# Two weight loads moved to ScalarE's queue, and one more chunk divided in token order, in a two-layer linear-attention kernel

## The chip, the cores and the metric

One core of a Trainium2 chip. The metric is the device time of one execution in microseconds (us), as the median of several executions. All runs quoted here are of the same state (fast).

## The reference, cut to what matters

```python
def _A_ref(x, wqkv, wo):                       # linear attention, 32 heads of 16
    q, k, v = split(x @ wqkv)
    phi = lambda t: where(t > 0, t + 1, exp(t)) + 1e-6
    pq, pk = phi(q), phi(k)
    kv  = einsum("bhsd,bhse->bhde", pk, v)
    z   = einsum("bhsd->bhd", pk)
    num = einsum("bhqd,bhde->bhqe", pq, kv)
    den = einsum("bhqd,bhd->bhq", pq, z)[..., None] + 1e-6
    return (num / den) @ wo                    # heads merged again

def _B_ref(x, w1, b1, w2, b2):                 # norm, w1, gelu, w2
    ...
x = x + _A_ref(norm(x), wqkv, wo);  x = x + _B_ref(norm(x), ...)     # layer 0
x = x + _A_ref(norm(x), wqkv, wo);  x = x + _B_ref(norm(x), ...)     # layer 1, same weights
```

x is 2048 tokens x 512 channels, the inner width of the second block is 1792, everything is bf16 outside.

## The kernel before

The program is scheduled by hand: a list per engine fixes the order of every operation (`ORDER`), a table says where an operation with a choice runs (`WAY`). A small planner walks these lists with a fixed duration for each operation; from that it takes the PSUM bank of every product (PSUM is the memory that TensorE's products go to; the program uses eight banks of it) and the semaphore waits, by which one engine waits for another. Tokens are handled in 16 tiles of 128, in four chunks. Tiles count from 0: the "fourth tile" is tile 3, and it is the fifth to be transposed. Where the prediction says "fourth transpose", it means that of tile 4, which comes just before.

The names that matter below: `PTA0_3` is the transpose on TensorE of the normalised tile 3 of layer 0, `tcA0_3` the copy of it out of PSUM by ScalarE, `K0_3` its four key products, `G0_3_0` its four products of normalised input and phi(k). `D` products make denominators, `ZR1` spreads layer 1's key sum over the partitions, `M1_x` joins the key-value matrix with the output weights, `WO1_x` is the attention's output, `PTB1_x` the second norm's transpose, `W11_...` the first MLP product of layer 1.

The loads at the start, and the two late weights (cut):

```python
dma("sp",  x0)                         # 128 KB, x tile 0
dma("act", x1)                         # 384 KB, x tiles 1 to 3
dma("sp",  wqkv[:, :, D:2*D])          # wk, 512 KB
load_chunk("act", 1, -98)              # 512 KB each
dma("act", wqkv[:, :, 0:D])            # wq, 512 KB
load_chunk("act", 2, -96)
load_chunk("act", 3, -95)
...
if st == 0:                            # after the first transposed tile has been copied
    late("wv", "wv", wqkv[:, :, 2 * D:3 * D], wsrc[:, :, 2 * D:3 * D], -88, 512, [tr])   # GpSimd issues
    late("wo", "wo", wo[:], A_wo.rearrange("(dt p) c -> p dt c", p=P), -87, 512, [tr])
```

The orders in the head (cut):

```
pe:   warm PTA0_0 PTA0_1 K0_0 K0_1 PTA0_2 PTA0_4 K0_2 G0_0_0 PTA0_3 ...
act:  x1 xc1 wq xc2 xc3 tcA0_0 tcA0_1 expk0_0 reluk0_0 tcA0_2 ...
pool: id0 id1 bdm0 neghalf b1z powA0_0 powA0_1 wv powA0_2 vepsA0_4 powA0_4 wo vepsA0_3 powA0_3 ...
dve:  ones statsA0_0 aggrA0_0 vepsA0_0 statsA0_1 statsA0_2 aggrA0_1 normA0_0 vepsA0_1 ...
```

The division by the denominators has two forms, chosen for each chunk (cut):

```python
if by_token(L, c):                                        # token order
    pool/dve: lr = pq * zrow                              # pz
    dve:      rd = reduce_add(heads(lr))                  # red
    dve:      rd = rd + 1e-6                              # den, 128x32
    dve:      rr = reciprocal(rd)                         # rec
    pool/dve: pq = pq * rr                                # pr
    sp:       DMA transpose of pq
else:                                                     # channel order
    pe:  d = zb^T pq                                      # D, 128x512
    act: lr = exp(-ln(d + 1e-6))                          # two instructions
    pool/dve: pq = pq * lr                                # pr
```

## Time and profile before

| | before |
|---|---|
| median of the first three runs | 330.97 us (330.16 to 331.24) |
| span of the profiled run | 328.4 us |
| TensorE busy | 320.1 us, 97% |
| first transpose starts / fourth tile's transpose starts | 6.02 / 12.67 us |
| last product ends | 325.90 us |

The profile's views are shown and read in the prediction below. One rule carries most of the reading: the modelled ends of pipelined matmuls overlap, so a stall of TensorE is read from starts. In this kernel a 512-wide product starts 0.216 us after the one before it; whatever the distance has above that is a stall (or half rate, at which it is 0.427 us; see e10).

A second view of the kernel before: ScalarE's part of the timeline up to its first copy. Columns: start, duration, engine (ACTq is the issue of a transfer by ScalarE), line, operation, output <- input, count, and in brackets the idle time before it and what ended it.

```profile
1.83 0.53 ACTq L626 DMA_DIRECT2D wqkv<-in_A_wqkv_dram  x1
2.39 1.22 ACTq L614 DMA_DIRECT2D t<-in_A_x_dram  x2
6.46 0.60 ACT L729 ACTIVATE t<-ps 128x512 bf16<-128x512 bf16 x1 [4.38 <-PE ps L719]
```

The last of five issues ends at 3.61 us, and the first copy waits for TensorE's transpose.

### The profile page before, as it was taken

The numbers are of one execution on the slowest core, as the hardware profiler recorded it, in microseconds if no ns is written. First come the engines' busy times: TensorE is split into PE (matmuls) and PEld (weight loads), VectorE is DVE, ScalarE is ACT, GpSimd is POOL, SyncE is SP. The second block draws the span as 40 slices with busy tenths as digits, with TensorE's granted clock in tenths as the row PEclk, the third lists the DMA queues.
The fourth block names the chain that finished last, engine by engine and source line by source line (L and its number), as shares of the span: only waits on it lengthen the run. The fifth ranks groups of instructions, "written<-read, shape, count | busy, mean of one in ns | idle before, by whom it ended". The sixth has DMA issues, their size and how long they took to land.

```text
span 328.4 us, 4737 instructions
## 1 busy us (share of the span) xinstructions
PE 320.1 (97%) x1696; PEld 159.1 (48%) x1726; DVE 211.9 (65%) x475; ACT 202.1 (62%) x343; POOL 146.8 (45%) x237
## 2 busy tenths in 40 slices
PE   6899999999999999999999999999999999999996
PEld 2344544576444444444444444458644444444444
DVE  5987757993664567564168889999688985300122
ACT  3899599588873764238974595859955250864300
POOL 4774566767335212753126725856654274000000
PEclk9999999999999999999999999999999999999999
DMA  7833770215022100322020200012033313300012
GB/s 257 271 65 66 229 254 0 50 29 69 17 47 45 22 1 18 64 48 48 2 48 0 50 17 1 18 32 51 16 82 80 79 21 80 96 0 2 16 44 68
DMA packets 45555, 19.71 MB, mean 60 GB/s; under 512 B 39196, under 2 KB 44572, under 8 KB 45532
## 3 DMA queue, kind: packets, MB, share of 16 engines
q1 hardware_dynamic: 41964, 12.21, 17.3%
q0 software_dynamic: 1056, 4.72, 4.2%
q10 hardware_dynamic: 2512, 2.49, 2.3%
q8 instruction: 13, 0.21, 0.3%
q14 instruction: 10, 0.08, 0.1%
HBM read 8.00 MB, written 2.10 MB: 31 GB/s over the span
## 4 chain that ended last, share of the span: by engine, by line
PE 90%; DVE 3%; ACT 2%; DMA 2%; issue 1%; POOL 0%
PE ps L1045 29%; PE ps L1083 28%; PE ps L1013 8%; PE ps L770 8%; PE ps L865 4%; PE ps L801 4%; PE ps L788 3%; PE ps L897 2%; DMA t<-in_A_x_dram 2%; PE ps L1070 1%; PE ps L989 1%; ACT eb L740 1%; DVE gtb L910 1%; PE ps L719 1%; PE ps L846 0%
## 5 line engine op out<-in xcount | busy, mean ns | idle before, releaser
L1051 ACT ACTIVATE gT<-ps,b1c 128x512 bf16<-128x512 f32 (+1 forms) x140 | 76.9, 601 | 56.9 <-PE ps L1045 53.0
L1045 PE MATMUL ps<-t,w 128*128 128x512 bf16 (+1 forms) x552 | 101.2, 336 | 0.3
L1083 PE MATMUL ps<-w,gT 128*128 128x512 bf16 x426 | 97.7, 379 | 0.5
L1045 PEld LDWEIGHTS ps<-t,w 128*128 128x128 bf16 x560 | 54.5, 98 | 43.7 <-ACT t L729 0.3
L1083 PEld LDWEIGHTS ps<-w,gT 128*128 128x128 bf16 x434 | 42.5, 98 | 50.3
L740 ACT ACTIVATE eb<-ps 128x512 bf16<-128x512 f32 x64 | 36.9, 602 | 8.4 <-PE ps L770 4.5
L683 POOL TENSOR_TENSOR rstd<-veps,neghalf 128x1 f32<-128x1 f32 x64 | 37.1, 585 | 6.5 <-DVE veps L681 3.0
L1093 DVE TENSOR_TENSOR outb<-ps,xsb 128x512 bf16<-128x512 f32 x15 | 10.3, 689 | 39.9 <-PE ps L1083 25.7
L671 DVE BATCH_NORM_STATS2 stats<-xsb 128x6 f32<-128x512 f32 x48 | 31.8, 679 | 0.3
L770 PE MATMUL ps<-wqkv,t 128*128 128x512 bf16 x125 | 31.1, 379 | 0.2
L751 ACT ACTIVATE rb<-ps 128x512 bf16<-128x512 f32 x45 | 26.6, 605 | 7.5 <-PE ps L770 3.9
L1013 PE MATMUL ps<-gtb,t 128*128 128x512 bf16 x125 | 30.6, 379 | 0.4 <-DVE gtb L881 0.2
L691 ACT ACTIVATE yb<-xsb,nmr,rstd 128x512 bf16<-128x512 f32 x21 | 16.9, 810 | 16.0 <-POOL nmr L688 15.9
L757 POOL TENSOR_TENSOR t<-eb,rb 128x512 bf16<-128x512 bf16 x14 | 16.8, 1201 | 12.2 <-DVE eb L753 7.5
L696 DVE TENSOR_SCALAR yb<-xsb,mv,rstd 128x512 bf16<-128x512 f32 x27 | 15.5, 578 | 8.8 <-POOL rstd L683 8.6
L997 POOL TENSOR_TENSOR t<-t,lr 128x512 bf16<-128x512 bf16 x13 | 15.3, 1180 | 12.7 <-ACT lr L993 12.3
L681 POOL TENSOR_SCALAR veps<-mv 128x1 f32<-128x1 f32 x29 | 8.0, 279 | 27.6 <-DVE mv L673 26.9
L753 DVE TENSOR_SCALAR eb<-eb 128x512 bf16<-128x512 bf16 x45 | 14.6, 333 | 8.5 <-ACT eb L740 8.5
L1089 DVE TENSOR_TENSOR xsb<-ps,xsb 128x512 f32<-128x512 f32 x16 | 11.0, 690 | 13.5 <-PE ps L1083 13.5
L1013 PEld LDWEIGHTS ps<-gtb,t 128*128 128x128 bf16 x128 | 12.4, 98 | 14.7 <-DVE gtb L881 0.7
L1213 ACT ACT_TABLE_LOAD x15 | 19.2, 1283 | 0.3
L770 PEld LDWEIGHTS ps<-wqkv,t 128*128 128x128 bf16 x128 | 12.1, 98 | 14.6 <-ACT t L729 0.6
(91 smaller groups left out, 390.5 us busy)
## 6 DMA issues: line engine op xcount, KB each, us to landing
w<-in_B_w_dram POOLq DMA_DIRECT2D x4, 896.0 KB, 7.0
out_dram<-outb SPq DMA_DIRECT2D x15, 128.0 KB, 1.8
t<-in_A_x_dram ACTq DMA_DIRECT2D x3, 512.0 KB, 8.3
t<-yb SPq DMA_TRANSPOSE x55, 2.5
wqkv<-in_A_wqkv_dram SPq DMA_DIRECT2D x1, 512.0 KB, 5.6
wqkv<-in_A_wqkv_dram ACTq DMA_DIRECT2D x1, 512.0 KB, 7.3
wqkv<-in_A_wqkv_dram POOLq DMA_DIRECT2D x1, 512.0 KB, 6.3
wo<-in_A_wo_dram POOLq DMA_DIRECT2D x1, 512.0 KB, 5.0
```

Source lines behind the costliest of these rows:

```text
L671: G.op("dve", lambda e: e.bn_stats(stats[:, s.slot, :], src()), 620, reads=src_keys, writes=[k + "s"], tiles=[s, *src_tiles], prio=prio, n ...
L683: G.op("pool", lambda e: e.tensor_tensor(rstd[:, s.slot:s.slot + 1], veps[:, s.slot:s.slot + 1], neghalf[:], op=ALU.pow), 570, reads=[k + ...
L691: G.op("act", lambda e: e.activation(yb[:, y.slot, :], src(), ACT.Identity, bias=nmr[:, s.slot:s.slot + 1], scale=rstd[:, s.slot:s.slot + 1]),
L740: G.op("act", lambda e: e.activation(eb[:, et.slot, :], bank(bt), ACT.Exp), 478, reads=[src_key], writes=[f"e{tag}"], tiles=[bt, et], prio ...
L751: G.op("act", lambda e: e.activation(rb[:, rt.slot, :], bank(bt), ACT.Relu), 478, reads=[src_key], writes=[f"r{tag}"], tiles=[bt, rt], pri ...
L757: lambda e: e.tensor_tensor(dst(), eb[:, et.slot, :], rb[:, rt.slot, :], op=ALU.add),
L770: ins = e.matmul(bank(b), lhsT=yTa(yT)[:, dt, k * P:(k + 1) * P], rhs=wqkv[:, dt, D:2 * D], start=(dt == 0), stop=(dt == DT - 1))
L1013: ins = e.matmul(bank(wb), lhsT=yTa(pq)[:, kt, k * P:(k + 1) * P], rhs=gtb[:, kt, :], start=(kt == 0), stop=(kt == DT - 1))
L1045: ins = e.matmul(bank(b, n), lhsT=w1[:, dt, ft * P:(ft + 1) * P], rhs=yTa(yT)[:, dt, k0 * P:k1 * P], start=(dt == 0), stop=(dt == DT - 1))
L1051: G.op("act", lambda e, ft=ft, b=b, k0=k0, k1=k1, n=n: e.activation(gT[:, g.slot, ft * 512 + k0 * P:ft * 512 + k1 * P], bank(b, n), ACT.Ge ...
L1083: ins = e.matmul(bank(b), lhsT=gT[:, g.slot, ft * 512 + k * P:ft * 512 + (k + 1) * P], rhs=w2[:, ft, :], start=(ft == 0), stop=(ft == FT - 1))
L1213: e.preload_act_table_set(sets[table])
```

## The change

The intent: take the two issues off GpSimd, where they stand between the norms that the first transposes wait for, and take four products and a transpose off TensorE, the engine that bounds the kernel. All orders and some 75 placements were redone along with it. The core of the diff, orders and placements cut:

```diff
         load_chunk("act", 3, -95)
+        dma("act", lambda e: e.dma_start(wqkv[:, :, 2 * D:3 * D], wsrc[:, :, 2 * D:3 * D]), ["wv"], prio=-94, name="wv", kb=512)
+        dma("act", lambda e: e.dma_start(wo[:], A_wo.rearrange("(dt p) c -> p dt c", p=P)), ["wo"], prio=-93, name="wo", kb=512)
 ...
-                    late("wv", "wv", wqkv[:, :, 2 * D:3 * D], wsrc[:, :, 2 * D:3 * D], -88, 512, [tr])
-                    late("wo", "wo", wo[:], A_wo.rearrange("(dt p) c -> p dt c", p=P), -87, 512, [tr])
 ...
-pe:   warm PTA0_0 PTA0_1 K0_0 K0_1 PTA0_2 PTA0_4 K0_2 G0_0_0 PTA0_3 ...
+pe:   warm PTA0_0 K0_0 PTA0_1 PTA0_2 K0_1 K0_2 PTA0_4 G0_0_0 PTA0_3 ...
-act:  x1 xc1 wq xc2 xc3 tcA0_0 tcA0_1 ...
+act:  x1 xc1 xc2 wq xc3 wv wo tcA0_0 reluk0_0 tcA0_1 ...
 ...
-  "TB0_3": "pe",   "den0_2": "tok", "den1_1": "tok", ...
+  "TB0_3": "dma",  "den0_2": "tok", "den0_3": "tok", "den1_1": "tok", ...
 ...   # the low half of layer 1's key sum gets a buffer of its own
-  G.op("dve", lambda e: e.tensor_tensor(zrow[:], zacc[:], dz[:], op=ALU.subtract), ..., writes=["zrow"], name="zlo")
+  zl = Tile(EB, "zlo")
+  G.op("dve", lambda e: e.tensor_tensor(eb[:, zl.slot, :], zacc[:], dz[:], op=ALU.subtract), ..., writes=["zlo"], name="zlo")
 ...   # the planner's caps on PSUM banks and its durations
-  N_K=4, N_N=2, dma issue 450, Z 595, KV 380, ZH 300
+  N_K=2, N_N=3, dma issue 540 (ScalarE) / 420, Z 400, KV 220, ZH 200
```

## The prediction

> **What bounds the kernel now.** I read the page first: busy shares, the 40 slices, the chain of work that ended last.
>
> ```profile
> PE 320.1 (97%) x1696; PEld 159.1 (48%) x1726; DVE 211.9 (65%) x475; ACT 202.1 (62%) x343; POOL 146.8 (45%) x237
> ...
> PE   6899999999999999999999999999999999999996
> ...
> PEclk9999999999999999999999999999999999999999
> ...
> PE 90%; DVE 3%; ACT 2%; DMA 2%; issue 1%; POOL 0%
> ```
>
> TensorE (PE) is busy nearly everywhere, at full clock, and carries 90% of the chain. But matmul ends are modelled, so busy time cannot tell a stall from a pipelined matmul. I therefore went to the timeline of TensorE alone and used start-to-start distances: four 128x512 matmuls in a row take 0.86 us (groups of four start at 16.58, 17.44 and 18.30), so 0.216 us each; a 256-wide one 0.109 us; a 128-wide one 0.056 us; the one-column ones 0.025 us.
>
> The program has, without the warm-up, 1308 matmuls of 512 columns, 252 of 256, 68 of 128 (36 transposes, 32 in the key-value product) and 88 of one column: 1308 x 0.216 + 252 x 0.109 + 68 x 0.056 + 88 x 0.025 = 282.5 + 27.5 + 3.8 + 2.2 = 316.0 us. The first real TensorE work starts at 6.02 us and the last ends at 325.9, so 319.9 us pass and only 3.9 are stalls. The span of 328.4 is then 6.0 (head) + 316.0 (streaming) + 3.9 (stalls) + 2.5 (tail: last addition and output).
>
> Where the stalls lie, from the same timeline:
>
> ```profile
> 6.02 0.40 PE L719 MATMUL ps<-idp,yb 128*128 128x128 bf16 x4 [0.38 <-DVE veps L681]
> 7.16 0.40 PE L719 MATMUL ps<-idp,yb 128*128 128x128 bf16 x4 [0.74 <-DVE veps L681]
> 7.40 1.89 PE L770 MATMUL ps<-wqkv,t 128*128 128x512 bf16 x8
> 9.45 0.40 PE L719 MATMUL ps<-idp,yb 128*128 128x128 bf16 x4 [0.16 <-DVE yb L696]
> 10.59 0.40 PE L719 MATMUL ps<-idp,yb 128*128 128x128 bf16 x4 [0.74 <-DVE yb L696]
> ...
> 11.68 1.03 PE L865 MATMUL ps<-pkb,yb 128*128 128x512 bf16 x4
> ...
> 199.53 0.39 PE L989 MATMUL ps<-t,zb 128*128 128x512 bf16 x1
> 200.13 0.39 PE L934 MATMUL ps<-dz,onesm 128*128 128x512 bf16 x1 [0.21 <-DVE dz L931]
> ...
> 212.83 1.47 PE L1013 MATMUL ps<-gtb,t 128*128 128x512 bf16 x6 [0.17 <-DVE gtb L881]
> ```
>
> By starts, 2.1 us go between 6.2 and 10.6 (0.91, 0.33, 0.90), where the first four transposes wait for norms; 1.2 us go at the passage from layer zero to layer one (0.25 before 199.53, 0.39 before 200.13, 0.24 near 205.3, 0.33 before 212.83), where VectorE is busy without a break; about 0.4 us in three small places before 50. Elsewhere the only jumps are of exactly 0.216 us, one every 10.8 us: a missing record each, not a stall. So the whole change can win only from head, passage and tail, or by taking work off TensorE.
>
> GpSimd in the head, which the change's title names:
>
> ```profile
> 6.11 0.55 POOL L683 TENSOR_TENSOR rstd<-veps,neghalf 128x1 f32<-128x1 f32 x1 [1.17 <-DVE veps L681]
> 7.36 0.98 POOL L640 DMA_DIRECT2D wqkv<-in_A_wqkv_dram  x1 [0.70 <-ACT t L729]
> 8.38 0.57 POOL L683 TENSOR_TENSOR rstd<-veps,neghalf 128x1 f32<-128x1 f32 x1
> ...
> 9.51 0.57 POOL L683 TENSOR_TENSOR rstd<-veps,neghalf 128x1 f32<-128x1 f32 x1
> 10.04 0.84 POOL L640 DMA_DIRECT2D wo<-in_A_wo_dram  x1
> ```
>
> The third rstd had its input at 7.17 (VectorE's veps) but started at 8.38: the issue of wv stood before it. Its norm ran at 8.98 and its transpose at 9.45.
>
> **What the Trainium skill says.** "DMA: Bandwidth & Descriptors", section "Issuing engines are not separate DMA queues": transfers from any engine run on the same 16 DMA engines, and another issuer saves only sequencer time. The trace agrees: x chunks and weights land 1.4 to 1.5 us apart whatever queue issued them (9.16, 10.66, 12.17 from ScalarE, 13.68, 15.07 from GpSimd), so moving wv and wo will not make the data come sooner; an issue costs 0.84 to 0.98 us on GpSimd and 0.45 to 0.61 on ScalarE. "Perfetto Trace Analysis", section "Per-instruction lifecycle", says that TensorE's end time is a model; the 0.379 us mean of a 512-wide matmul against its 0.216 us spacing agrees. "SBUF — State Buffer", section "Who interferes with whom": a VectorE instruction with two SBUF inputs contends with GpSimd's reads. The trace agrees: the zb product took 1.46 us at 198.01 beside a GpSimd addition at 197.77 to 198.92, and 0.69 us at 40.35, where it began first and the GpSimd addition beside it took 1.42 us rather than 1.15.
>
> **The change, part by part.**
>
> 1. wv and wo issued by ScalarE. GpSimd loses 0.98 + 0.84 us of issue in the head; ScalarE gains 2 x 0.6 = 1.2 us, ending near 4.9 us, before its first copy at 6.46. So it is free there. VectorE's order changes too: the first norm goes one statistic earlier. Rebuilt with the durations above: x's first tile at 3.2, rstd 4.4 to 4.9, norm to 5.4, first transpose near 5.5 (was 6.02); K of tile 0 can start when wk has landed (6.86) near 6.95; second norm later than before (statistics of tile 3 precede it), transpose near 7.85; third rstd near 8.0, but its norm now follows a statistic and ends near 9.05, transpose 9.1; K 1 to 10.2, K 2 to 11.1; fourth transpose 11.1, first G to about 12.2 to 12.4. Before, the same set of work was done at 12.67. Gain 0.35 us, not the 1.2 us by which GpSimd is relieved, since VectorE takes over as the limit.
>
> 2. Layer zero's last chunk ("layer one" by the title's count) divides by its denominators in token order. That removes four 128x512 matmuls (the D products), 4 x 0.216 = 0.86 us of TensorE; eight ScalarE instructions of 0.63 to 0.70; it adds four reductions (0.69), four small additions and reciprocals on VectorE and four DMA transposes (2.4 us each to landing). Chunk 3's output product lies near 120 us and its queries near 56, so the added latency has tens of microseconds to hide in. The 0.86 is on the bound and counts in full.
>
> 3. One transpose of layer zero's second norms (tile 3) moves from TensorE to DMA: 4 x 0.056 = 0.22 us, counts in full.
>
> 4. The split sum of layer one gets its own buffer, K may hold two PSUM banks instead of four, the denominators three instead of two; every engine's order and some 70 placements are redone. In the passage the zb product comes two instructions sooner after zs, and the last phi of K leaves GpSimd (1.15 us there, 0.42 on VectorE), so Z and zs come sooner: I take 0.5 of the 1.2 us as saved.
>
> 5. The tail: the last two half-width products now stand side by side instead of around a full one. The last half still ends in one 0.42 us addition and one output transfer of about 2 us: 0.
>
> Sum: 0.35 + 0.86 + 0.22 + 0.5 = 1.9 us. Against it I set 0.4 us for stalls that a new order brings where there are none now. Net 1.5 us, 0.5%: 330.97 - 1.5 = 329.4 us.
>
> **Rivals.** (a) ScalarE's queue blocks on seven transfers, so the first copy is late and the head grows. Against it: its five issues took 0.45 to 0.61 us each without waiting for any landing. If it happened, up to 3 us worse: 332 to 333. (b) The first half of w1 is now issued after a GpSimd product that ended at 52.6 us before, instead of at 35. A transfer of 896 KB took 5 to 10 us to land, 6.8 for the one that was issued alone late; so it lands near 59.5, and the first W1 product started near 63.8. There are about 4 us of slack, but DMA transposes start at 59.25 and took up to 4 us beside bulk traffic. If they collide: 1 to 2 us worse, near 331. (c) VectorE, continuous from 200 to 212, gets more work and the passage grows: the net is then zero, about 331. (d) The scheduler's orders were good already and the passage loses all its 1.2 us, and the head gains 1 us: 327.5.
>
> **Range and chances.** TensorE still streams 314.9 us, and head start and tail cost at least 7.9 us more; with no stall at all the span would be 322.8, so 5.6 us (1.7%) below now. Faster by over 2% (under 324.4) is thus practically closed. Slower by over 2% (over 337.7) needs 6 us of new stalls in a kernel that has 3.9. Predicted 329.4 us, 8 in 10 between 327.8 and 331.3; faster 0.01, within 2% 0.97, slower 0.02.
>
> **What would show each step.** Part 1: in the timeline no DMA issue among GpSimd's norms, the first G product done before 12.5 us; landings of wv and wo still near 13.7 and 15.1. Parts 2 and 3: TensorE's count 8 lower by the program (1688 or so by records), D products 12 instead of 16. Part 4: the stalls between 195 and 213 sum to about 0.7 us. Part 5: 2.5 us from the last matmul to the end. I am wrong if ScalarE's first copy is later than 6.5, if TensorE waits for w1 or for a transpose near 60, if a new gap of over half a microsecond stands anywhere between 13 and 195 us, or if the passage's stalls grow.

## The result, and the profile after

| | before | after |
|---|---|---|
| median (six runs each) | 330.93 us | 330.68 us |
| lowest to highest | 330.16 to 331.24 | 329.75 to 331.32 |
| span of the profiled run | 328.4 | 328.0 |
| fourth tile's transpose starts | 12.67 | 13.38 |
| last product ends | 325.90 | 325.49 |

The ratio is 0.9995, with a 95% interval of 0.9976 to 1.0014: no change. Here and below a ratio is the mean time of one kernel's fast runs over the mean of the other's of the same rounds, so it is not quite the ratio of the medians quoted. The forecast of 329.4 us was 1.3 us too low, though its range holds the result.

The page of the profile after: busy time, then the chain's shares.

```profile
PE 320.7 (98%) x1718; PEld 158.2 (48%) x1718; DVE 217.9 (66%) x491; ACT 199.3 (61%) x333; POOL 148.0 (45%) x234
...
PE 91%; DVE 4%; ACTq 2%; ACT 1%; POOL 0%; issue 0%; DVEq 0%
```

The count of TensorE's records is higher than before although the program has eight instructions fewer: before lacks 30 records, after lacks none. What is new is ACTq in the chain: ScalarE's issuing of transfers, which was not in it before. The chain of waits of the kernel after, followed back from the end of its first 16 us, says where (start, duration, what):

```profile
3.08 0.65 ACTq L613
...
3.75 2.13 ACTq L628
...
5.91 1.61 ACTq L629
...
7.57 0.61 ACT t L730
```

L613 is the last chunk of x, L628 is wv, L629 is wo. The fifth issue took 0.65 us; the sixth took 2.13 and the seventh 1.61, and ScalarE did nothing else meanwhile. Its first copy started at 7.57 us, not 6.46, and with it the first K products. TensorE's side of the same stretch:

```profile
5.57 0.61 PE L720 MATMUL ps<-idp,yb 128*128 128x128 bf16 x4
8.22 1.04 PE L771 MATMUL ps<-wqkv,t 128*128 128x512 bf16 x4 [2.04 <-ACT t L730]
...
10.44 2.02 PE L771 MATMUL ps<-wqkv,t 128*128 128x512 bf16 x8 [0.73 <-ACT t L730]
...
13.38 0.39 PE L720 MATMUL ps<-idp,yb 128*128 128x128 bf16 x4
```

The first transpose is earlier, as forecast (5.57 for 5.5). Then TensorE waits 2.30 us by starts for the copy, and 0.89 us more before the second K. The transpose of tile 3 comes 0.71 us later than before.

The products that were to go did go. Groups of TensorE by line and form, the D products, before:

```profile
L989 PE MATMUL ps<-t,zb 128*128 128x512 bf16 x15 | 5.7, 380 | 0.1
```

and after (before lacks one record of its 16):

```profile
L991 PE MATMUL ps<-t,zb 128*128 128x512 bf16 x12 | 4.5, 379 | 0.0
```

The passage from layer 0 to layer 1 in the timeline of TensorE after:

```profile
208.71 1.03 PE L789 MATMUL ps<-wqkv,t 128*128 128x512 bf16 x4
209.78 1.04 PE L945 MATMUL ps<-wo,kvb 128*128 128x512 bf16 x4
...
213.79 3.44 PE L1015 MATMUL ps<-gtb,t 128*128 128x512 bf16 x14
217.50 1.04 PE L1015 MATMUL ps<-gtb,t 128*128 128x512 bf16 x4 [0.28 <-DVE xsb L1020]
```

By starts: 209.78 - 208.71 - 4 x 0.216 = 0.20 us of stall before M1. The 14 output products from 213.79 take 3.71 us where 14 x 0.216 = 3.02 would do; the 0.69 are a stall of 0.24 inside them at 216.19 and one of 0.44 before 217.50. With 0.30 before ZR1 (at 199.18) and 0.09 before WO1_0 the passage has 1.27 us of stalls; before it had 1.20. The first two places of before (D1 and KV1) are gone, and two new ones stand further on.

What VectorE did there, timeline of VectorE after:

```profile
206.51 0.17 DVE L973 TENSOR_SCALAR rd<-rd 128x32 f32<-128x32 f32 x1
...
207.83 1.16 DVE L973 TENSOR_SCALAR rd<-rd 128x32 f32<-128x32 f32 x1
...
212.80 1.13 DVE L973 TENSOR_SCALAR rd<-rd 128x32 f32<-128x32 f32 x1
```

and GpSimd after, beside the second and third:

```profile
207.80 1.15 POOL L967 TENSOR_TENSOR lr<-t,zrow 128x512 f32<-128x512 bf16 x1
...
212.63 1.26 POOL L758 TENSOR_TENSOR t<-eb,rb 128x512 bf16<-128x512 bf16 x1 [1.54 <-DVE eb L754]
```

One addition of 1e-6 to 32 numbers per partition takes 0.17 us where it starts before the GpSimd product (206.51; the product beside it started at 206.56) and 1.16 and 1.13 us when the product has just started. Both long ones end 0.03 to 0.04 us after that product (207.83 + 1.16 = 208.99 against 208.95; 213.93 against 213.89): the small instruction waited for the whole of the large one. Before had three such in its passage, of 0.79, 0.68 and 0.73 us. Behind the first of after, with a reciprocal between, stand the kvb products of VectorE, on which M1 waits; right behind the second stands the residual addition, which frees the bank that WO1_4 and WO1_5 need.

The account between the two profiled runs, by starts: head +0.71; stalls near 28 and 49 us -0.24 (0.31 before, 0.07 after); D products and transpose -1.08 (the stretch from the first output product of layer 0 to the first G1_1 took 129.22 us before and 128.14 after); passage +0.07; one new stall of 0.09 near 265. Sum -0.45, against -0.41 measured at the last product's end.

### The profile page after: what moved, and what is told of

It reads as the page before. It is cut to its first block, busy times and chain, and to the rows that moved or that the text cites. A ratio compares the mean times of both kernels' runs of the same rounds, so it can differ in the third digit from the quotient of the medians.

```text
span 328.0 us, 4752 instructions
## 1 busy us (share of the span) xinstructions
PE 320.7 (98%) x1718; PEld 158.2 (48%) x1718; DVE 217.9 (66%) x491; ACT 199.3 (61%) x333; POOL 148.0 (45%) x234
## 4 chain that ended last, share of the span: by engine, by line
PE 91%; DVE 4%; ACTq 2%; ACT 1%; POOL 0%; issue 0%; DVEq 0%
PE ps L1047 30%; PE ps L1085 29%; PE ps L771 9%; PE ps L1015 7%; PE ps L867 4%; PE ps L789 3%; PE ps L899 3%; PE ps L802 3%; PE ps L1072 1%; DVE rd L973 1%; ACTq L628 1%; PE ps L991 1%; PE ps L848 1%; DVE xsb L1020 1%; ACTq L613 1%; ACTq L629 0%
## 5 line engine op out<-in xcount | busy, mean ns | idle before, releaser
L1053 ACT ACTIVATE gT<-ps,b1c 128x512 bf16<-128x512 f32 (+1 forms) x140 | 78.3, 602 | 65.6 <-PE ps L1047 64.9
L684 POOL TENSOR_TENSOR rstd<-veps,neghalf 128x1 f32<-128x1 f32 x64 | 38.4, 604 | 7.2 <-DVE veps L682 3.7
L771 PE MATMUL ps<-wqkv,t 128*128 128x512 bf16 x128 | 31.7, 379 | 2.8 <-ACT t L730 2.8
L1015 PE MATMUL ps<-gtb,t 128*128 128x512 bf16 x128 | 31.7, 379 | 0.4 <-DVE xsb L1020 0.3
L752 ACT ACTIVATE rb<-ps 128x512 bf16<-128x512 f32 x43 | 25.1, 606 | 3.9 <-PE ps L771 3.7
L1032 POOL TENSOR_TENSOR xsb<-xsb,b2b 128x512 f32<-128x512 f32 x17 | 20.2, 1195 | 6.1 <-DVE yb L697 6.0
L697 DVE TENSOR_SCALAR yb<-xsb,mv,rstd 128x512 bf16<-128x512 f32 x29 | 16.3, 564 | 8.5 <-POOL rstd L684 8.4
L692 ACT ACTIVATE yb<-xsb,nmr,rstd 128x512 bf16<-128x512 f32 x19 | 15.3, 811 | 10.2 <-POOL nmr L689 10.1
L1091 DVE TENSOR_TENSOR xsb<-ps,xsb 128x512 f32<-128x512 f32 x16 | 11.0, 689 | 15.3 <-PE ps L1085 15.2
L789 PE MATMUL ps<-wqkv,t 128*128 128x512 bf16 x80 | 20.2, 379 | 0.0
L979 POOL TENSOR_TENSOR t<-t,rr 128x512 bf16<-128x512 bf16 x13 | 14.1, 1091 | 10.6 <-DVE rr L975 9.7
```

The costliest lines, as they stand in the source:

```text
L684: G.op("pool", lambda e: e.tensor_tensor(rstd[:, s.slot:s.slot + 1], veps[:, s.slot:s.slot + 1], neghalf[:], op=ALU.pow), 570, reads=[k + ...
L752: G.op("act", lambda e: e.activation(rb[:, rt.slot, :], bank(bt), ACT.Relu), 478, reads=[src_key], writes=[f"r{tag}"], tiles=[bt, rt], pri ...
L771: ins = e.matmul(bank(b), lhsT=yTa(yT)[:, dt, k * P:(k + 1) * P], rhs=wqkv[:, dt, D:2 * D], start=(dt == 0), stop=(dt == DT - 1))
L789: ins = e.matmul(bank(b), lhsT=yTa(yT)[:, dt, k * P:(k + 1) * P], rhs=wqkv[:, dt, 0:D], start=(dt == 0), stop=(dt == DT - 1))
L1015: ins = e.matmul(bank(wb), lhsT=yTa(pq)[:, kt, k * P:(k + 1) * P], rhs=gtb[:, kt, :], start=(kt == 0), stop=(kt == DT - 1))
L1032: G.op("pool" if on_pool else "dve", lambda e: e.tensor_tensor(xsb[:, st, :], xsb[:, st, :], b2b[:], op=ALU.add), 1120 if on_pool else 600 ...
```

## The experiments

Fifteen runs of twelve kernels, the changed one among them; each has the kernel before on the same chip beside it (330.37 to 331.0 us). All results are correct. "Tile 3's transpose" is the start of PTA0_3 in the profiled run; before has 12.67, after 13.38.

| kernel | chip | median (range), us | ratio to before (95%) | tile 3's transpose |
|---|---|---|---|---|
| e1_sp | 3 | 329.54 (328.57 to 331.38) | 0.9969 (0.9944 to 0.9993) | 13.05 |
| e2_pool | 3 | 329.37 (328.62 to 330.32) | 0.9970 (0.9951 to 0.9989) | 12.25 |
| e3_before_act | 3 | 331.57 (330.25 to 332.54) | 1.0020 (0.9997 to 1.0043) | 14.01 |
| e4_act_late | 3 | 328.94 (328.12 to 329.81) | 0.9947 (0.9928 to 0.9966) | 11.76 |
| e5_wide_x | 12 | 332.39 (331.76 to 333.02) | 1.0062 (1.0045 to 1.0078) | 15.60 |
| e6_no_den | 12 | 328.47 (327.93 to 329.26) | 0.9943 (0.9926 to 0.9960) | 11.81 |
| e7_fill | 12 | 329.15 (328.63 to 329.82) | 0.9963 (0.9947 to 0.9978) | 12.59 |
| e8_wo_late | 12 | 329.22 (329.02 to 329.61) | 0.9966 (0.9952 to 0.9981) | 11.89 |
| e9_best | 13 | 332.50 (331.54 to 333.77) | 1.0063 (1.0042 to 1.0084) | 13.21 |
| e10_after_again | 13 | 332.23 (330.77 to 333.32) | 1.0047 (1.0025 to 1.0070) | 15.24 |
| e11_late_again | 13 | 329.24 (328.22 to 329.87) | 0.9960 (0.9942 to 0.9978) | 11.71 |
| e12_no_den_only | 13 | 330.89 (330.10 to 331.33) | 1.0010 (0.9994 to 1.0026) | 14.48 |
| e13_fill_after | 13 | 330.74 (330.14 to 331.64) | 1.0010 (0.9991 to 1.0030) | 13.13 |
| e14_no_den_again | 13 | 329.02 (328.39 to 329.86) | 0.9957 (0.9942 to 0.9973) | 13.76 |
| e15_after_third | 13 | 332.60 (329.52 to 333.61) | 1.0055 (1.0020 to 1.0090) | 14.80 |

The theory: ScalarE cannot get rid of its sixth and seventh transfer while the earlier ones are still in its queue, and that costs the head about what the other parts win. The rivals: the new order of norms and transposes is what is late; or the gain is lost in the passage.

### Who issues: e1_sp, e2_pool

e1 gives both issues to SyncE, behind the first copied tile; e2 gives them back to GpSimd, in the changed kernel's orders.

```diff
-act: x1 xc1 xc2 wq xc3 wv wo tcA0_0 ...
+act: x1 xc1 xc2 wq xc3 tcA0_0 ...
+sp:  x0 wk wv wo b2 b1 ...                              # e1, after the first copied tile
+pool: ... powA0_0 id1 powA0_1 wv powA0_2 vepsA0_4 powA0_4 wo ...   # e2
```

> The changed kernel, with the value and output weights issued by SyncE's queue after the first transposed copy, nothing else changed. Theory 1 (ScalarE's queue fills: the changed trace has 2944 packets of 1 KB issued and 612 done when the value weights' issue ends, 3456 and 1175 when the output weights' ends, about 2300 outstanding both times, and the first PSUM copy stands behind it): ScalarE's first copy starts near 6.0 us instead of 7.57, the first K product near 7.0 instead of 8.22, the fourth tile's transpose near 12.3 instead of 13.38, span 327.0 and time about 329.6 (0.997 of before). Theory 2 (the head is late because of the new VectorE order and K 0 going before the second transpose): the fourth tile's transpose stays near 13.4, time 330.7.

> The changed kernel, with the value and output weights issued by GpSimd between the first norms as in the kernel before: only the title's first part undone. Theory 1: first copy near 6.0 us, fourth tile's transpose near 12.7 as before, span near 327.4, time about 330.0. Theory 2: no gain in the head, time 330.7. If the GpSimd issues cost what the title assumes (two rstd's late by 1 us each) the head is 0.4 us later than in the run with SyncE.

Measured: 329.54 and 329.37 us, 1.5 to 1.6 us under the kernel before and near what the prediction had wanted from the whole change. On SyncE the two issues took 0.38 and 0.51 us, on GpSimd 0.98 and 0.83. With the issues in either place, the change is thus worth about what was forecast for all of it. e1's profiled run was the slowest of its six: TensorE ran at half rate up to 10.4 us and a DMA transpose was late, both of which come back below.

### The move alone, on the kernel before: e3_before_act

```diff
 # the kernel before
-pool: ... powA0_1 wv powA0_2 vepsA0_4 powA0_4 wo vepsA0_3 ...
+pool: ... powA0_1 powA0_2 vepsA0_4 powA0_4 vepsA0_3 ...
-act: x1 xc1 wq xc2 xc3 tcA0_0 ...
+act: x1 xc1 wq xc2 xc3 wv wo tcA0_0 ...
```

> The kernel before, with only the value and output weights moved to ScalarE's queue behind x: the title's first part alone. Theory 1: the value weights' issue takes about 2 us and the output weights' about 1.6 (against 0.5 to 0.6), ScalarE's first copy goes from 6.46 to about 7.6, the head grows by about 1.0 us, span 329.4, time about 332.0 (1.003). Theory 2: issues of about 0.6 us each, no loss, and with rstd 2 earlier 0.3 us gained.

Measured: 331.57 us, ratio 1.0020 (the interval just holds 1). Timeline of ScalarE in e3:

```profile
3.66 2.20 ACTq L627 DMA_DIRECT2D wqkv<-in_A_wqkv_dram  x1
5.89 1.60 ACTq L628 DMA_DIRECT2D wo<-in_A_wo_dram  x1
```

The same two long issues in the old orders, so the new order of norms is not the cause. The transpose of tile 3 came at 14.01, 1.34 us later than before, part of it through half rate in the first K products.

### The same engine, later: e4_act_late, e11_late_again

Nothing differs from the changed kernel but the place of the two issues in ScalarE's list.

```diff
-act: x1 xc1 xc2 wq xc3 wv wo tcA0_0 reluk0_0 tcA0_1 expk0_0 tcA0_2 reluk0_1 expk0_1 tcA0_4 reluk0_2 ...
+act: x1 xc1 xc2 wq xc3 tcA0_0 reluk0_0 tcA0_1 expk0_0 tcA0_2 reluk0_1 wv expk0_1 tcA0_4 wo reluk0_2 ...
```

> The changed kernel, the two weights still issued by ScalarE but after its first copies (near 9 and 11 us), when part of x has landed. Theory 1 (it is the full queue, not ScalarE as the issuer): each issue takes 0.5 to 0.6 us, first copy near 6.0 us, head about 0.5 us later than with SyncE because 1.1 us of issue stand between the first phi instructions; span near 327.4, time about 330.0. If a ScalarE issue of these two is slow in itself (their pattern), they stay near 2 us and the time stays at 330.7 or worse.

> The version with both weights late on ScalarE, once more on the same chip: 0.9947 of before in its first measurement, expected again between 0.994 and 0.997; passage stalls stay near 1.25 us in sum, since it does not touch them.

Measured: 328.94 us on one chip, 329.24 on another, ratios 0.9947 and 0.9960. Timeline of ScalarE in e4:

```profile
5.65 0.60 ACT L729 ACTIVATE t<-ps 128x512 bf16<-128x512 bf16 x1 [3.57 <-PE ps L719]
...
9.90 0.37 ACTq L627 DMA_DIRECT2D wqkv<-in_A_wqkv_dram  x1
...
11.10 0.37 ACTq L628 DMA_DIRECT2D wo<-in_A_wo_dram  x1
```

The same two transfers on the same queue cost 0.37 us each, 5 to 6 us later. The first copy starts at 5.65 us instead of 7.57, tile 3's transpose at 11.76, 0.91 us before the kernel before's. Between the profiled runs of after and e4 this head is 13.38 - 11.76 = 1.62 us and the span 1.6 us (328.0 and 326.4); the passage has the same five stalls in both, and the planner gives every product the same PSUM bank in both (as in e1, e2, e5 and e8), so a reshuffled plan is not behind it. So it is neither ScalarE nor the transfers as such, but issuing them while the five earlier loads are still in the queue (which limit is met stays open, see e5). In medians, e11 is 3.0 us under the changed kernel of the same chip (e10, 332.23), with intervals far apart; half rate in e10's head is part of that.

### One of the two: e8_wo_late

```diff
+act: x1 xc1 xc2 wq xc3 wv tcA0_0 reluk0_0 tcA0_1 expk0_0 tcA0_2 reluk0_1 expk0_1 tcA0_4 wo reluk0_2 ...
```

> The changed kernel with only the seventh transfer (output weights) issued after the first copies; the value weights stay sixth behind x. Theory 1: their issue still takes about 2.1 us and ends near 5.9, but the first copy, ready near 5.9, follows at once: first copy near 6.0, head as in the version with both late less 0.5 us of issue, time about 329.0. So the loss would be due to the seventh transfer alone. If any full queue holds ScalarE longer than the issue shows, first copy near 7 and 330.

Measured: 329.22 us. wv still took 2.27 us to issue, but that ended at 5.90 us, and the first transposed tile was there at 6.04; the copy started at 6.08. The sixth transfer's wait is hidden by time in which ScalarE has nothing to do. It is the seventh that costs.

### What the queue counts: e5_wide_x

x loaded with four rows to a partition, so in packets of 4 KB instead of 1 KB, and the output written back to match.

```diff
-x_dram[c * 512:(c + 1) * 512, :].rearrange("(k p) d -> p k d", p=P)
+x_dram[c * 512:(c + 1) * 512, :].rearrange("(p k) d -> p k d", k=4)
```

> The changed kernel with the seven transfers on ScalarE's queue as they are, but each partition takes four neighbouring rows of x (and the output is written back the same way), so an x chunk is 128 packets of 4 KB instead of 512 of 1 KB; the bytes are the same. If the queue is full by number of packets (about 2300 outstanding), at most 2050 are ever issued on it: the two weight issues take 0.4 to 0.6 us each, the first copy starts near 6.0, time about 329.0 to 329.6. If it is full by bytes, the issues stay near 2.1 and 1.6 us and the first copy near 7.5, time 330.7.

Measured: 332.39 us, worse than before, and neither of the two outcomes expected. wv was issued in 0.48 us, wo still took 1.63. The records of the transfers tell how much was issued and not yet done. In the changed kernel 2332 packets of 1 KB were outstanding when wv's issue ended and 2281 when wo's did (2316 and 2258 in e3, 2286 after wv in e8); in the kernel before, which never waited, the peak after five issues was 2082. That looks like a limit near 2300, though in e15 the two waits ended at about 2230 and 2160. And in e5 wv went through without a wait with 1403 packets (2540 KB) outstanding, and wo's wait ended at 1831 packets (2716 KB). So neither a fixed number of packets nor a fixed number of bytes explains both. What exactly is full stays open. The time itself says nothing about the queue: x's first tile landed at 4.02 us in e5 (2.91 to 3.32 in the others, 3.30 in after), and the head ran at half rate.

### The small additions: e6_no_den, e12_no_den_only, e14_no_den_again

The addition of 1e-6 to the token-order denominators is taken out (they are sums of phi, each of which already carries its 1e-6; the result stays correct). e6 and e14 do it on top of e4, e12 in the changed kernel.

```diff
-G.op("dve", lambda e, d=d: e.tensor_scalar(rd[:, d.slot, :], rd[:, d.slot, :], 1e-6, None, op0=ALU.add), 100, ..., name=f"den{tag}")
```

> The version with the two weights issued late by ScalarE (328.9 us, fourth tile's transpose at 11.76), without the 20 VectorE additions of 1e-6 to the token-order denominators (these sums are over 2048 keys, so the output does not change). In the passage two of these small additions took 1.16 and 1.13 us instead of 0.17, each beside a GpSimd product, just before the stalls at 209.8 (0.20) and at 216.2 and 217.5 (0.24 and 0.44). Theory (the passage is bound by VectorE, and it is these blocked small instructions that moved its stalls): the stalls at the M and the fifth and sixth output products shrink from 0.88 to under 0.3 us together, span 325.8, time about 328.3. Rival (some other instruction of VectorE gets blocked in their place, or TensorE waits for something else): stalls stay near 1.2 us in sum, time 328.9.

> The changed kernel without the 1e-6 additions, the weights still sixth and seventh on ScalarE's queue. If head and passage are two separate losses: head as in the changed kernel (fourth tile's transpose near 13.4, issues of 2.1 and 1.6 us), passage stalls near 0.4 us, 0.85 us better than the changed kernel, 329.7. If the passage's gain was an accident of the other timing, stalls stay near 1.2 us and the time at 330.5.

> The version with both loads issued late on ScalarE and without the twenty additions of 1e-6, which gave 328.47 us (ratio 0.9943) on another chip. If its gain is real and not one chip's: ratio to the kernel before between 0.992 and 0.996. If the gain belonged to the chip: 0.998 or more.

Measured: e6 328.47 us, the best median of all. Timeline of TensorE in e6, the place of the stretched output products:

```profile
212.60 4.05 PE L1008 MATMUL ps<-gtb,t 128*128 128x512 bf16 x18
216.48 0.39 PE L715 MATMUL ps<-idp,yb 128*128 128x128 bf16 x4
```

All 18 output products in a row: 216.48 - 212.60 = 3.88 = 18 x 0.216. The stalls before M1, WO1_4 and WO1_5 are gone and the passage has 0.29 + 0.10 = 0.40 us left of 1.27. In e12 it has 0.38 while the head's waits are the changed kernel's (2.08 and 1.92 us), so the two losses are separate. e12 is 1.3 us faster than e10, the changed kernel on the same chip, more than the 0.9 us of the passage; the head differs too between their executions (below), and the 329.7 us expected were missed by 1.2. In e6 and e12 the planner's banks differ from after's for 26 products only, all of them behind the passage (from WO1_14_0 on), so other banks do not explain the passage's gain. As a whole e6 is not clearly faster than e4 (intervals 0.9926 to 0.9960 and 0.9928 to 0.9966, on different chips); its profile shows what it removes, and also a late DMA transpose of 0.59 us that e4's does not have. e14, the same kernel as e6 on chip 13, gave 0.9957: the gain over the kernel before is not one chip's, and e14 is under the changed kernel (332.60). But e11, which keeps the additions, has 0.9960 on the same chip: in the median their removal on top of the late weights shows nothing. The passage of e14 also shows that the rival of e6's expectation can come true. Timelines of TensorE, VectorE and GpSimd in e14:

```profile
205.92 0.40 PE L917 MATMUL ps<-gtb,wqkv 128*128 128x128 bf16 x4 [0.35 <-DVE gtb L907]
...
200.77 1.38 DVE L753 TENSOR_TENSOR t<-eb,rb 128x512 bf16<-128x512 bf16 x1
...
200.72 1.16 POOL L962 TENSOR_TENSOR lr<-t,zrow 128x512 f32<-128x512 bf16 x1 [2.36 <-ACT zrow L875]
```

Here another instruction of VectorE, an addition with two inputs, took 1.38 us instead of 0.41 (e6) beside a GpSimd product that started 0.05 us before it, and a stall of 0.52 us by starts stands before a KV product: 0.91 us in the passage instead of 0.40. The profiled runs of e1 and e13 have the same collision and 2.23 us of stalls in the passage, with the additions. So the removal is worth 0.9 to 1.3 us of stalls between like executions, and the passage is not the same in every execution.

### One more step that failed: e9_best

e6 with ZR1 one place later in TensorE's list, since its stall of 0.29 us was left.

```diff
-pe: ... Z1_3 G1_2_2 G1_3_1 D1_0_0 ZR1 G1_3_2 G1_2_0 ...
+pe: ... Z1_3 G1_2_2 G1_3_1 D1_0_0 G1_3_2 ZR1 G1_2_0 ...
```

> Both repairs together (weights late on ScalarE, no 1e-6 additions) and the product that spreads z over the partitions placed after one more group of G products, to fill the one stall of 0.29 us left in the passage. If the passage is only short of filler there, that stall goes and no other comes: span 325.8 in a run without a slow DMA transpose, time about 328.0 (0.993 of before, 0.994 of the changed kernel). Rival: the later z row delays the denominators and a stall of the same size comes back at the output products: 328.4.

Measured: 332.50 us. ZR1's stall is gone, but layer 1's first W1 products wait again and again (0.90, 0.59 and eight times 0.29 us between 222 and 236). The planner's own assignment of PSUM banks, printed for both kernels, points to why:

```
e6: ZR1 in bank 4, Q1_2_3 in bank 7; W1 tiles of layer 1 in banks 0 1 3 2 0 3 1 0 2 3 0 2 1 3
e9: ZR1 in bank 0, Q1_2_3 in bank 0; W1 tiles of layer 1 in banks 2 1 2 3 2 1 2 3 1 3 1 2 3 2
```

One swap of two products changed who takes which bank for the next 20 us, and a query tile sat in bank 0 when the MLP began: it had three banks to turn over instead of four, and each product waited for the gelu of an earlier one. The head ran partly at half rate in this run too (tile 3's transpose at 13.21 for e6's 11.81), so not all of the 4 us is from this; and that the banks are the cause is read from the planner and the waits together, not tried by itself.

### The changed kernel again, and half rate: e10_after_again, e15_after_third

```diff
 # no edit: the changed kernel
```

> The changed kernel itself once more, on the same chip as the repairs: 330.5 (0.999 to 1.000 of before) if the result stands; first copy near 7.5, the weights' issues near 2.1 and 1.6 us, passage stalls near 1.25 us in sum.

> The changed kernel unaltered, a third time. So far 0.9995 and 1.0047 on two chips. The two issues again take 2.0 to 2.2 and 1.5 to 1.9 us. If its time is set by whether the head runs at half rate: a profile with K products at 0.216 us goes with a time near 330.7, one with 0.43 us with a time near 332; anything else says that the difference between the chips lies elsewhere.

Measured on chip 13: 332.23 and 332.60 us, ratios 1.0047 and 1.0055, both intervals above 1; the 330.5 us expected of e10 were missed. On this chip the change costs 1.5 to 1.9 us more than on the first. The two issues took 2.03 and 1.57 us (e10), 2.53 and 1.64 (e15), much as before. What differs is TensorE's rate. Timeline of TensorE in e10:

```profile
8.09 1.89 PE L771 MATMUL ps<-wqkv,t 128*128 128x512 bf16 x4 [2.02 <-ACT t L730]
9.77 1.06 PE L720 MATMUL ps<-idp,yb 128*128 128x128 bf16 x8
11.15 3.17 PE L771 MATMUL ps<-wqkv,t 128*128 128x512 bf16 x8 [0.32 <-ACT t L730]
```

Four K products take 9.77 - 8.09 = 1.68 us, where they took 0.88 in the profile of after: twice as long. The same holds up to 13.9 us. The mean granted clock of this run is recorded as 1.0, so only the distances of starts show it. In e15 the first four K products are at full rate and the next ones at half (0.427 us apart, up to 13.3 us), and its profiled execution took 331.17 us, between the two values expected. Between the profiles of after and e15 tile 3's transpose is 1.42 us later and the span 1.4 us longer; for e10 it is 1.86 us, plus 0.70 of a late DMA transpose, against 2.6. So in these profiles the time follows the head. Half rate is not chip 13's alone: K products at half rate stand in the profiles of e1 and e3 (chip 3) and e5 (chip 12) too.

### Keeping TensorE busy in the wait: e7_fill, e13_fill_after

Dummy products that read constants and whose result nobody uses: 4 and 3 behind the first two transposes on top of e4 (e7); 5 and 2 in the changed kernel (e13).

```diff
-pe: warm PTA0_0 K0_0 PTA0_1 PTA0_2 K0_1 ...
+pe: warm PTA0_0 fill0 K0_0 PTA0_1 fill1 PTA0_2 K0_1 ...
```

> The version with the weights late, plus seven dummy 512-column products in the waits of the head (four after the first transposes, three after the second). In the profiled runs of the version with SyncE and of the kernel before with ScalarE the first K products came 0.427 us apart instead of 0.216 and those runs were the slower ones; in the others not. Theory (after the waits of the head TensorE's clock is sometimes granted at half for a while, which makes the spread of times of 1.7 to 2.8 us): with the waits filled, K products come 0.216 apart and the spread of six times shrinks to about 1.2 us, median 328.7. Rival (spread comes from elsewhere): spread unchanged; and if the dummies delay the K products, 0.3 us worse.

> The changed kernel with five dummy 512-wide products after the first transpose and two after the second, so that TensorE is not idle while it waits for ScalarE's first copy. If the half rate that some profiles show in the head comes from these waits and makes part of the loss: the first K products are spaced 0.216 us in the profile, the fourth tile's transpose starts near 13.4 us, and the time is 0.5 to 1.8 us shorter than the changed kernel's of the same chip where that one is cold, with a narrower spread. If the half rate is no part of it, or comes whatever TensorE did just before: same time as the changed kernel within 0.3 us, or up to 0.5 us longer, since the dummies can themselves delay the first K product when they run at half rate (5 x 0.43 = 2.1 us against a wait of 2.3).

Measured: e7 329.15 us, no gain over e4's 328.94 and 329.24; there the wait is short and the K products of both profiled runs are at full rate without help. The spread of six times was 1.2 us, as expected (1.7 in e4 and e11). The dummies themselves delayed the head (tile 3's transpose at 12.59 for e4's 11.76). e13 330.74 us (330.14 to 331.64), 1.9 us under the unaltered kernel (332.60; 329.52 to 333.61). Timeline of TensorE in e13:

```profile
5.43 1.24 PE L662 MATMUL ps<-onesm 128*128 128x512 bf16 x5
7.97 1.04 PE L779 MATMUL ps<-wqkv,t 128*128 128x512 bf16 x4 [1.30 <-ACT t L738]
...
10.19 2.02 PE L779 MATMUL ps<-wqkv,t 128*128 128x512 bf16 x8 [0.30 <-ACT t L738]
```

The K products come at full rate (1.04 and 2.02 us for four and eight, like after's; e10 had 1.89 and 3.17). The issues of wv and wo were as long as ever (1.86 and 1.66), so the wait itself is untouched, and with the dummies the change is worth nothing, not a loss (1.0010).

That the dummies did this by keeping TensorE at full rate is argued, not shown. In e13's profile the warm-up products had reached full rate at 4.86 us, before the first dummy at 5.43. e14 had reached it at 4.87 too, waited 2.3 us without dummies and fell back to half at 8.5, which fits. But in e1 and e9 half rate stands behind a wait of only 1.1 to 1.2 us, and in after full rate follows a wait of 2.3 us that began at half rate. So the length of the wait does not decide it. The profiled executions of e13 and e15 are also equally long (329.4 us each): the head of e13 is 1.67 us shorter, but a late DMA transpose (0.64) and the passage (2.23 for 1.25) took that back. The 1.9 us is a difference of medians, between kernels whose intervals (up to 1.0030 and from 1.0020) just overlap.

## Why the prediction was wrong

**Step 1, the head: failed, and it decides.** The step said that ScalarE's two issues cost "2 x 0.6 = 1.2 us, ending near 4.9 us, before its first copy at 6.46. So it is free there." They cost 2.13 + 1.61 us and ended at 7.52. The 0.6 us was the duration of the first five issues, carried over to the sixth and seventh: the queue was taken to have no end. Instead of a gain of 0.35 us the head lost 0.71. The other half of the step was right and even too careful: with the issues out of the way (e4) tile 3's transpose came at 11.76 us, a gain of 0.91. The landings were as forecast as well (wv 13.8 and wo 15.2 us). Rival (a) was the right one. It was dismissed because five issues had not waited, which says nothing of seven. Its price, "up to 3 us worse: 332 to 333", was met only on chip 13 (332.2 and 332.6), and there by chance: 1.5 to 1.9 us of it came on top, with half rate in the head. The queue alone cost the 1.62 us between after and e4.

**Steps 2 and 3, D products and transpose: right in size.** 0.86 + 0.22 = 1.08 forecast, 1.08 measured over the stretch that holds them. The added latency of token order was hidden, as forecast.

**Step 4, the passage: failed.** Forecast 0.5 of 1.2 us saved; measured 1.27 us of stalls. The zb product did come sooner (ended at 198.51 for 199.47; 0.61 of these 0.96 us the kernel was ahead already, by the last Z product), and the stalls of D1 and KV1 went. But VectorE still lost 2 us to small additions blocked behind GpSimd products (1.7 before, over three of them), now right ahead of what M1 and WO1 wait for, and the stalls moved on to there. The prediction had quoted the blocking of products with two inputs and did not ask which of VectorE's other instructions GpSimd holds up; e6 and e12 show the term: 1.27 us of stalls with the additions, 0.40 and 0.38 without (0.91 in e14, where a larger instruction was blocked).

**Step 5, the tail:** right, 2.5 us in both.

**The 0.4 us set aside for new stalls:** 0.09 came, outside head and passage, and 0.24 of old ones went.

Together: 1.06 us too good in the head, 0.57 in the passage, 0.55 too bad in small stalls (0.31 too many forecast and 0.24 saved). The forecast gain of 1.5 us becomes 1.5 - 1.06 - 0.57 + 0.55 = 0.42, and the profiled pair shows 0.41. The range was wide enough for that on the first chip (330.68 against 327.8 to 331.3); it did not hold chip 13's medians, since half rate in the head was not thought of at all; e10 shows every product up to 13.9 us at double length. One reading was loose, without effect: missing records come 10.8 us apart only from about 99 us on, 6 to 12 us apart before.

Rival (b) did not occur: the halves of w1 landed at 53.97 and 58.07 us and no stall stands near 60. Rival (c), the passage growing through VectorE, named the right engine, but the passage grew by 0.07 us only. Rival (d) got its better head only once the issues were moved.

**What stays open.** What it is in the queue that fills (e5). Why half rate lasts in some executions and not in others, and whether the dummies end it. Why DMA transposes issued at 17 to 25 us are late in some runs: about 0.6 to 1.5 us of TensorE stall between 22 and 28 us in e1 and e6 to e13 (1.51 in e11), none in after, e2 to e5, e14 and e15. Why VectorE and GpSimd collide in the passage of some executions (e1, e13, e14). Whether the removal of the additions gains in the median what it gains in the trace (0.9957 in e14, 0.9960 in e11).

## What to carry to other kernels

The price of an issue, read from a few of them, need not hold for the next: here the first five took 0.45 to 0.65 us, the sixth and seventh 1.6 to 2.1. Count what is outstanding before another load goes to an engine that is soon to compute, or put the load behind that engine's first work. When a stall disappears from one product, look for the next instruction on the engine that fed it, since in a kernel this tight the wait tends to move on. And where a fixed order decides buffers, one swap can change the banks of products far behind it: compare the bank lists, not only the order.

## What the Trainium skill lacked or had wrong

- "DMA: Bandwidth & Descriptors", section "Issuing engines are not separate DMA queues", says that another issuer saves only sequencer time, "usually small relative to the DMA itself". For a queue as full as here (about 2070 packets of 1 KB outstanding when the sixth issue began, 2300 when it ended) this misleads: the issues took 2.13 and 1.61 us instead of 0.45 to 0.65 (and 0.37 once most had landed, e4), and ScalarE did nothing else meanwhile. "Perfetto Trace Analysis", section "Per-instruction lifecycle", has a possible half of the mechanism: the profiled time of such an issue is the wait for and use of the descriptor generator, not the movement of data, and there is a descriptor buffer that can fill. It does not say that the issue then waits, and gives no size. No run here shows that this buffer is what fills; they show that the wait ends neither at a fixed packet count nor at fixed bytes (2332 packets of 1 KB; 1831 packets with 2716 KB).
- "SBUF — State Buffer", section "Who interferes with whom", was right and under-used here: it says that a tensor_scalar can enter a mode that shares a port pair with GpSimd and that the later one "fully blocks". The trace agrees: 0.17 us where the small addition started first, 1.16 and 1.13 where a GpSimd product had, ending 0.03 to 0.04 us after it. It lacks the remark that very small instructions lose most in proportion, nearly seven times their length here.
- "TensorE: Matmul & The Clock Gate", section "Part 1: The HAM clock gate", agrees in its two rates (0.427 and 0.216 us for 512 columns, as in e10 and after). It speaks of a busy window of about 3.4 us that runs freely, so that the moment varies from run to run; in e10 half rate lasted to 13.9 us after warm-up products from 1.5 us on, with TensorE waiting for much of the stretch between, and in e14 it came back at 8.5 us after a wait of 2.3 us. What decides it the runs do not show. Its caution that clock records are not to be trusted alone also agrees: the record of e10 says 1.0.
- The same page, section "Back-to-back issue gap", gives about 131 ns for sustained 512-wide products and about 216 for isolated ones. At full rate the runs here have 216 ns, over some 1300 of them.
- I found no page that tells why DMA transposes that mostly take 2.4 to 2.5 us to land take up to 5.0 (e11) now and then, in after (3.37) and before (3.96) too.
